# One block of attention products a pair in place of three, between the units of a Strassen MLP

## The chip, the cores and the metric

The kernel runs on one core of a Trainium2 chip. The metric is the device time of one execution in microseconds (us), as the median of several runs. A profile is one execution with the hardware profiler on; it gives a start and a duration for each instruction of each engine: TensorE (PE, and PEld for its weight loads), VectorE (DVE), ScalarE (ACT), GpSimd (POOL), SyncE (SP, which here issues DMAs).

## What is computed

A retention layer (attention without softmax, with a decay per head) feeds an MLP with a PReLU.

```python
# q, k, v: (8 batches, 8 heads, 576 positions, 64), all fp32
scores = q @ k.T / 8
ret = scores * where(i >= j, gamma[h] ** (i - j), 0)
x = (ret @ v), heads side by side            # (4608 tokens, 512)
h = x @ w_in                                 # (4608, 2048)
out = (max(h, 0) + alpha * min(h, 0)) @ w_out  # (4608, 512)
```

## The kernel before

**Attention.** Two heads make a pair; a batch has 4 pairs, so there are 32 of them, numbered n. A sequence is cut into 9 chunks of 64 positions. Inside a chunk the retention is worked out from scores; what lies in earlier chunks comes through a running state, a 64 x 64 sum of k and v products per head, decayed from chunk to chunk. A pair therefore has these steps:

- `load_pair`: SP loads `kx`, `qx` (to be transposed), `kn` and `vn`; two buffers of each.
- `scale_pair`: decay factors go onto `qx` (POOL, line 524) and `vn` (ScalarE, 529). `transposes`: `kT`, `qT` on VectorE (535).
- `pair_scores`: 18 products `kT` by `qT` into PSUM tiles `ps` (552); ScalarE copies `qT` into `mt` (555); VectorE masks the scores into `mt` (560).
- `pair_states`: 16 products `kn` by `vn` into `pu` (571); ScalarE copies and VectorE adds up the running sums `su` (576 to 584). `pair_sums` copies `su` into the free half of `vn` (590).
- `pair_values`: 18 products of `vn` (values and sums, 128 rows) by `mt` (chunk scores and q, 128 rows) into `pv` (601); ScalarE copies `pv` into the MLP's input `xb` (610). One product thus yields the chunk's own part and that of the state.

Scores and states are 64*64 products that use quarters of TensorE's array, values are 128*64, MLP products 128*128. In fp32 one product is two instructions on TensorE.

**MLP.** 256 tokens make a block kb. From block 2 on, each of both matrix products is a 2 x 2 block product in 7 products with sums and differences of the operands (Strassen-Winograd); `combine_x` makes those of `xb` on POOL (449). A block has 8 units. A unit (`mlp_unit`) has 28 instructions into the PSUM tiles `ph` with tags `psh0` and `psh1` (line 463), then VectorE turns `ph` into `g` (474 to 485), and `mlp_out` issues the 14 instructions of the unit before it into `po` (381). After a block's last unit `out_block` adds `po` up on VectorE (367, 368) and SP sends two DMAs of 128 rows (371).

**PSUM** has 8 banks: two for attention (tag `psa`, through `ps_tile`), one each for `psh0` and `psh1`, four for `po`.

**Order.** The first 157 us (batches 0 and 1, blocks 0 and 1, and the preparation of the weights) are written out by hand under `manual_schedule`; there, too, pairs 4 to 7 go through the functions above. Then `queue` holds the MLP units that are ready, and a loop over the 24 pairs of batches 2 to 7 issues scores, some units, states, some units, transposes of the next pair and values, some units (`cuts` has the numbers; 2, 1 and 1 as a rule). A scheduler places these instructions on their engines; TensorE's come out in the order of the program, VectorE's nearly so. After a batch, `enqueue(b)` adds the blocks that it completed, so each batch's attention runs between the MLP units of the batch before it. The last 24 units have no attention beside them.

Of the kernel before, what the change touches and what calls it, by code (L numbers as in the profile page):

```python
# [18 lines left out]
def kernel(  # L19
# [49 lines left out]
    def half(x):  # L69
        return slice(x * C, (x + 1) * C)  # L70
# [36 lines left out]
    def load_pair(n):  # L107
        b, c = pairs[n]
        kx, qx, kn = [nat.tile([P, S], FP32, tag=t, name=f"{t}_{n}") for t in ("kx", "qx", "kn")]
        kx, qx = [t.rearrange("p (n r) -> p n r", r=32) for t in (kx, qx)]  # L110
        kn = kn.rearrange("p (j d) -> p j d", d=D)
        vn = nat.tile([P, 2, NJ, D], FP32, tag="vn", name=f"vn_{n}")
        load_sq(kx, k, b, c)
        load_sq(qx, q, b, c)
        for t, src in ((vn, v), (kn, k)):
            for h2 in range(2):
                load_head(t[half(1 - h2), h2] if t is vn else t[half(1 - h2)], src, b, 2 * c + h2)
        for h2 in range(2):

            nc.scalar.copy(vn[half(h2), h2, 0], zero[half(h2)])  # L120
        return kn, kx, qx, vn
# [233 lines left out]
    def out_block(kb, po):  # L355
        p1, p2, p6, p7, p5, p3, p4 = [po[n // 2][:, n % 2, :] for n in range(7)]

        osb = ring.tile([P, 2, 2, HM], FP32, tag=f"o{kb % 2}", name=f"osb_{kb}")
        s12 = wraw.tile([P, 2, HM], FP32, tag="wa", name=f"s12_{kb}")
        u3 = wraw.tile([P, HM], FP32, tag="wa", name=f"u3_{kb}")  # L360
        s1, u2 = s12[:, 0], s12[:, 1]
        nc.scalar.copy(s1, p1)
        for o, x, y, op in ((osb[:, 0, 0], p2, s1, ALU.add), (u2, p6, s1, ALU.add),
                            (u3, p7, u2, ALU.add), (s1, p5, u2, ALU.add),
                            (osb[:, 1, 1], p5, u3, ALU.add),
                            (osb[:, 0, 1], p3, s1, ALU.add)):
            nc.vector.tensor_tensor(out=o, in0=x, in1=y, op=op)  # L367
        nc.vector.tensor_tensor(out=osb[:, 1, 0], in0=p4, in1=u3, op=ALU.add)
        for m in range(2):
            t0 = kb * TB + m * P  # L370
            nc.sync.dma_start(out[t0:t0 + P, :], osb[:, m].rearrange("p x f -> p (x f)"))
# [134 lines left out]
    def pop_units(n):  # L506
        for _ in range(min(n, len(queue))):
            kb, i = queue.pop(0)
            mlp_unit(kb, i)
            if i == NU // 2 and kb + 1 < NKB and ready[kb + 1] <= done[0]:  # L510
                combine_x(kb + 1)
# [5 lines left out]
    def ps_tile(shape, name):  # L517
        return ps_a.tile(shape, FP32, tag="psa", name=name)

    def scale_pair(n):  # L520
        c = pairs[n][1]
        qx, vn = loaded[n][2:]
        qh = qx.rearrange("p (j x) r -> p j x r", x=2)
        nc.gpsimd.tensor_tensor(out=qh, in0=qh,  # L524
                                in1=tabx[:, None, c, :, None].to_broadcast([P, NJ, 2, 32]),
                                op=ALU.mult)
        for h2 in range(2):
            x = half(1 - h2)
            nc.scalar.activation(vn[x, h2], vn[x, h2], ACTF.Copy, scale=tabv[x, c:c + 1])  # L529

    def transposes(n):
        kT = attn.tile([P, S], FP32, tag="kT", name=f"kT_{n}")
        qT = attn.tile([P, S], FP32, tag="qT", name=f"qT_{n}")
        for src, dst in ((loaded[n][1], kT), (loaded[n][2], qT)):
            nc.vector.transpose(dst, src.rearrange("p n r -> p (n r)"))
        return kT, qT

    def chunk(j):
        return slice(j * C, (j + 1) * C)
# [3 lines left out]
    def pair_scores(n, kT, qT):  # L543
        c = pairs[n][1]

        mt = attn.tile([P, 2 * S], FP32, tag="at", name=f"mt_{n}").rearrange(
            "p (h j s) -> p h j s", h=2, s=C)
        ps = [ps_tile([P, NM, C], f"ps{p2}_{n}") for p2 in range(2)]
        for j in range(NJ):
            for h2 in range(2):  # L550
                x = (1 - h2, h2)[j % 2]
                nc.tensor.matmul(ps[j % 2][half(x), j // 2], kT[half(h2), chunk(j)],  # L552
                                 qT[half(h2), chunk(j)], start=True, stop=True)
        for h2 in range(2):
            nc.scalar.copy(mt[half(h2), h2].rearrange("p j s -> p (j s)"), qT[half(h2)])
        for p2 in range(2):
            for h2 in range(2):
                h, to, x = 2 * c + h2, half(1 - h2), (1 - h2, h2)[p2]
                nm = NM - p2
                nc.vector.scalar_tensor_tensor(  # L560
                    out=mt[to, h2, p2::2], in0=ps[p2][half(x), 0:nm], scalar=th[to, 3, h:h + 1],
                    in1=mask[to, None, :].to_broadcast([C, nm, C]), op0=ALU.mult, op1=ALU.mult)
        return mt

    def pair_states(n, kn, vn):
        c = pairs[n][1]
        ps = [ps_tile([P, NM - 1, D], f"pu{p2}_{n}") for p2 in range(2)]
        for j in range(NJ - 1):
            for h2 in range(2):
                x = (h2, 1 - h2)[j % 2]  # L570
                nc.tensor.matmul(ps[j % 2][half(x), j // 2], kn[half(1 - h2), j],  # L571
                                 vn[half(1 - h2), h2, j], start=True, stop=True)
        su = attn.tile([P, S], FP32, tag="kT", name=f"su_{n}")[:, 0:S - D].rearrange(
            "p (j d) -> p j d", d=D)
        g1, g2 = gch[:, 0, c:c + 1], gch[:, 1, c:c + 1]
        nc.scalar.copy(su[:, 0::2], ps[0])
        for h2 in range(2):
            nc.vector.scalar_tensor_tensor(
                out=su[half(h2), 1::2], in0=su[half(h2), 0::2], scalar=g1[half(h2)],
                in1=ps[1][half(1 - h2)], op0=ALU.mult, op1=ALU.add)  # L580
        for j in range(3, NJ - 1, 2):
            nc.vector.scalar_tensor_tensor(out=su[:, j], in0=su[:, j - 2], scalar=g2,
                                           in1=su[:, j], op0=ALU.mult, op1=ALU.add)
        nc.vector.scalar_tensor_tensor(out=su[:, 2::2], in0=su[:, 1:NJ - 3:2], scalar=g1,  # L584
                                       in1=ps[0][:, 1:], op0=ALU.mult, op1=ALU.add)
        return su

    def pair_sums(vn, su):
        for h2 in range(2):
            nc.scalar.copy(vn[half(h2), h2, 1:], su[half(h2)])  # L590

    def pair_values(n, vn, mt):
        b, c = pairs[n]
        w = TB // C

        j1 = -b * NJ % w or w
        j1 += w if NJ - j1 > 6 else 0
        pv = [ps_tile([P, (j1, NJ - j1)[i], C], f"pv{i}_{n}") for i in range(2)]
        for j in range(NJ):
            for h2 in range(2):  # L600
                nc.tensor.matmul(pv[j >= j1][half(h2), j - (j1 if j >= j1 else 0)],  # L601
                                 vn[:, h2, j], mt[:, h2, j], start=True, stop=True)
        j = 0
        while j < NJ:
            kb, o = divmod(b * NJ + j, w)
            if kb not in xb:
                xb[kb] = ring.tile([P, NCC, TB], FP32, tag=f"x{kb % NRING}", name=f"xb_{kb}")
            m, i = min(w - o, NJ - j), j >= j1
            j0 = j - (j1 if i else 0)
            nc.scalar.copy(xb[kb][:, c, o * C:(o + m) * C].rearrange("p (j s) -> p j s", s=C),  # L610
                           pv[i][:, j0:j0 + m])
            j += m
# [276 lines left out]
    enqueue(0)  # L889
    enqueue(1)  # L890

    for n, (b, c) in enumerate(pairs):
        if n <= last:
            continue
        if n == last + 1:
            pop_units(1)
        if n + 1 < len(pairs) and n + 1 not in loaded:
            loaded[n + 1] = load_pair(n + 1)
        kn, _, _, vn = loaded[n]
        share = -(-len(queue) // (NPAIR - c))  # L900
        cuts = [(share + i) // 3 for i in range(3)][::-1]
        kT, qT = turned.pop(n)
        mt = pair_scores(n, kT, qT)
        pop_units(cuts[0])
        pair_sums(vn, pair_states(n, kn, vn))
        pop_units(cuts[1])
        if n + 1 < len(pairs):
            scale_pair(n + 1)
            turned[n + 1] = transposes(n + 1)
        pair_values(n, vn, mt)  # L910
        del loaded[n]
        pop_units(cuts[2])
        if c == NPAIR - 1:
            enqueue(b)
    pop_units(len(queue))
    while pend:
        mlp_out()
# [28 lines left out]
```

## Time and profile before

| | |
|---|---|
| median of 12 runs | 1025.8 us (1024.52 to 1027.35) |
| profiled execution | 1025.64 us, of which the span of instructions is 1023.9 us |
| granted TensorE clock | 0.996 |
| PE busy | 1008.5 us, 98% |
| DVE busy | 768.0 us, 75% |
| ACT busy | 268.9 us |
| POOL busy | 179.2 us |

The span runs from the first to the last instruction; the run's time is 1.7 us longer. "Busy" sums the durations of an engine's instructions, and matmuls overlap, so a PE busy share near 100% says that TensorE nearly always had work in flight, not that it ran at its peak. Which engine sets the end is read from the chain that ended last: it follows the last instruction back, step by step, to what released it.

### The profile page before, as it was taken

The numbers are of one execution on the slowest core, as the hardware profiler recorded it, in microseconds if no ns is written. First come the engines' busy times: TensorE is split into PE (matmuls) and PEld (weight loads), VectorE is DVE, ScalarE is ACT, GpSimd is POOL, SyncE is SP. The second block draws the span as 40 slices with busy tenths as digits, with TensorE's granted clock in tenths as the row PEclk, the third lists the DMA queues.
The fourth block names the chain that finished last, engine by engine and source line by source line (L and its number), as shares of the span: only waits on it lengthen the run. The fifth ranks groups of instructions, "written<-read, shape, count | busy, mean of one in ns | idle before, by whom it ended". The sixth has DMA issues, their size and how long they took to land.

```text
span 1023.9 us, 23109 instructions
## 1 busy us (share of the span) xinstructions
PE 1008.5 (98%) x9385; PEld 890.9 (87%) x9385; DVE 768.0 (75%) x2038; ACT 268.9 (26%) x605; POOL 179.2 (17%) x201
## 2 busy tenths in 40 slices
PE   6999999999999999999999999999999999999998
PEld 5766668999999999999999999999999999999997
DVE  6769967787878787776868787878787777667665
ACT  4656652223222222122122221222222211000000
POOL 5656675200200010100010000200020001010000
PEclk8999999999999999999999999999999999999999
DMA  9975743223323222112113222222222100000000
GB/s 240 241 190 147 185 77 90 48 57 59 67 38 67 48 47 56 25 47 45 40 30 67 48 55 43 63 48 56 48 48 57 24 22 2 22 1 21 1 21 22
DMA packets 229307, 64.30 MB, mean 63 GB/s; under 512 B 214336, under 2 KB 222544, under 8 KB 229200
## 3 DMA queue, kind: packets, MB, share of 16 engines
q1 hardware_dynamic: 227088, 62.29, 26.8%
q8 instruction: 74, 1.21, 0.5%
q10 hardware_dynamic: 2112, 0.53, 0.3%
q14 instruction: 33, 0.27, 0.1%
HBM read 53.35 MB, written 9.44 MB: 61 GB/s over the span
## 4 chain that ended last, share of the span: by engine, by line
PE 98%; DMA 1%; DVE 0%; issue 0%; ACT 0%; SPq 0%; DVEq 0%
PE ph L463 40%; PE po L381 38%; PE ph L419 6%; PE po L398 6%; PE pv L601 3%; PE ps L552 2%; PE pu L571 2%; DMA w_out<-in_k_dram 1%; PE pt L642 0%; PE pv L720 0%; PE ps L661 0%; PE pv L709 0%; DVE pa L668 0%; PE pu L681 0%; DVE s L367 0%
## 5 line engine op out<-in xcount | busy, mean ns | idle before, releaser
L381 PE MATMUL po<-w_out,g 128*128 128x256 f32 x1792 | 407.8, 379 | 0.0
L381 PEld LDWEIGHTS po<-w_out,g 128*128 128x128 f32 x1792 | 330.8, 190 | 39.7
L474 DVE TENSOR_TENSOR g<-ph,g 128x256 f32<-128x256 f32 (+1 forms) x512 | 187.9, 388 | 184.4 <-ACT g L469 112.6
L463 PE MATMUL ph<-xb,w_in 128*128 128x128 f32 x2048 | 277.7, 279 | 0.0
L463 PEld LDWEIGHTS ph<-xb,w_in 128*128 128x128 f32 x2048 | 253.1, 192 | 8.2 <-issue 0.5
L463 PE MATMUL ph<-xt,w_in 128*128 128x128 f32 x1536 | 213.3, 275 | 0.0
L463 PEld LDWEIGHTS ph<-xt,w_in 128*128 128x128 f32 x1536 | 192.1, 192 | 0.0
L469 ACT COPY g<-ph 128x128 f32<-128x128 f32 x128 | 33.9, 265 | 396.4 <-PE ph L463 374.3
L485 DVE TENSOR_TENSOR g<-g 128x128 f32<-128x128 f32 x512 | 126.9, 289 | 7.8
L479 DVE SCALAR_TENSOR_TENSOR g<-g 128x512 f32<-128x512 f32 x128 | 91.8, 717 | 3.9
L477 DVE TENSOR_SCALAR g<-g,alpha 128x256 f32<-128x256 f32 x256 | 85.0, 374 | 3.7
L524 POOL TENSOR_TENSOR qx<-qx,tabx 128x576 f32<-128x576 f32 x28 | 32.9, 1174 | 309.8 <-DMA qx<-in_q_dram 254.6
L419 PE MATMUL ph<-xb,w_in 128*128 128x256 f32 x256 | 61.6, 397 | 0.8 <-ACT xb L728 0.8
L560 DVE SCALAR_TENSOR_TENSOR mt<-ps,th,mask 64x320 f32<-64x320 f32 (+1 forms) x112 | 57.8, 516 | 4.5 <-PE ps L552 2.7
L419 PEld LDWEIGHTS ph<-xb,w_in 128*128 128x128 f32 x256 | 50.0, 198 | 11.0 <-issue 3.2
L398 PE MATMUL po<-w_out,g 128*128 128x512 f32 x128 | 58.6, 599 | 0.9 <-DVE g L435 0.9
L449 POOL TENSOR_TENSOR xt<-xb 128x256 f32<-128x256 f32 x16 | 11.6, 727 | 214.7 <-PE ph L463 202.4
L449 POOL TENSOR_TENSOR xt<-xb,xt 128x256 f32<-128x256 f32 x32 | 23.6, 738 | 143.0 <-ACT xb L610 142.3
L529 ACT ACTIVATE vn<-vn,tabv 64x576 f32<-64x576 f32 x56 | 43.3, 773 | 15.3 <-DMA vn<-in_v_dram 14.7
L398 PEld LDWEIGHTS po<-w_out,g 128*128 128x128 f32 x128 | 23.4, 190 | 24.5 <-issue 22.9
L590 ACT COPY vn<-su 64x512 f32<-64x512 f32 x56 | 34.5, 616 | 37.8 <-DVE su L584 37.2
L610 ACT COPY xb<-pv 128x256 f32<-128x256 f32 (+3 forms) x84 | 22.6, 321 | 78.8 <-PE pv L601 78.7
(122 smaller groups left out, 688.6 us busy)
## 6 DMA issues: line engine op xcount, KB each, us to landing
out_dram<-osb SPq DMA_DIRECT2D x36, 256.0 KB, 2.3
kx<-in_k_dram SPq DMA_DIRECT2D x112, 72.0 KB, 2.6
qx<-in_q_dram SPq DMA_DIRECT2D x112, 72.0 KB, 2.5
vn<-in_v_dram SPq DMA_DIRECT2D x56, 144.0 KB, 3.2
kn<-in_k_dram SPq DMA_DIRECT2D x56, 144.0 KB, 3.2
raw<-in_moe_w_in_dram SPq DMA_DIRECT2D x24, 256.0 KB, 4.1
raw<-in_moe_w_out_dram SPq DMA_DIRECT2D x10, 512.0 KB, 4.6
w_in<-in_moe_w_out_dram SPq DMA_DIRECT2D x6, 512.0 KB, 5.6
```

The source lines that it names most:

```text
L381: nc.tensor.matmul(acc[kb][n // 2][:, n % 2, :], g[:, x, :], w_out[i][:, y, :], start=(i == 0 and n % 2 == 0), stop=(i == NU - 1 and (n % ...
L398: nc.tensor.matmul(acc[kb][m], g[:, 2 * x + m], w_out[i][:, 2 * x:2 * x + 2].rearrange("p x f -> p (x f)"), start=(i == 0 and x == 0), sto ...
L419: nc.tensor.matmul(ph[:, x], w_in[i // UST][:, cc // 2 * 2 + x, i % UST, cc % 2], xb[kb][:, cc], start=(cc == 0 and x == 0), stop=(cc == N ...
L449: nc.gpsimd.tensor_tensor(out=o, in0=x0, in1=x1, op=ALU.subtract)
L463: nc.tensor.matmul(ph[m][:, o], w_in[i // UST][:, l, i % UST, cc], r[:, cc], start=(n in (0, 3) and cc == 0), stop=(n in (2, 6) and cc == ...
L474: nc.vector.tensor_tensor(out=o, in0=x0, in1=x1, op=ALU.add)
L477: nc.vector.tensor_scalar(g[:, 4 + 2 * m:6 + 2 * m], g[:, 2 * m:2 * m + 2], 0.0, alpha[:, fc:fc + 1], ALU.min, ALU.mult)
L479: nc.vector.scalar_tensor_tensor(out=g[:, 0:4].rearrange("p x t -> p (x t)"), in0=g[:, 0:4].rearrange("p x t -> p (x t)"), scalar=0.0, in1 ...
L485: ins = nc.vector.tensor_tensor(out=g[:, o, :], in0=g[:, x0, :], in1=g[:, x1, :], op=op)
L529: nc.scalar.activation(vn[x, h2], vn[x, h2], ACTF.Copy, scale=tabv[x, c:c + 1])
L560: nc.vector.scalar_tensor_tensor(out=mt[to, h2, p2::2], in0=ps[p2][half(x), 0:nm], scalar=th[to, 3, h:h + 1], in1=mask[to, None, :].to_bro ...
L590: nc.scalar.copy(vn[half(h2), h2, 1:], su[half(h2)])
```

## The change

The loop over pairs gives way to a loop over units, which calls `joint(n)` after 25 of them.

- `joint(n)` issues the values of pair n-1, then one last score chunk of pair n, then (in `pair_front`) the other 16 score products and the 16 state products of pair n, all in one stretch on TensorE.
- Values and the last score chunk go into tiles of the tags `psh0` and `psh1`, which are those of `ph`; `extra` is the last 64 columns of the second one. Scores and states of a pair share two banks of `psa`.
- `pair_front` traces the copies of `qT` into `mt`, the two masks of the last chunk and the four others. The running sums (`running_sums`, split out of `pair_states`, and `pair_sums`) and the scaling and transposes of the next pair (`operands`) go into the list `later`; the loop takes one entry after each unit, though none after the first unit of a block.
- The places: with nq units in a batch's queue, units c * nq // 4 + 2 for c = 0 to 3, counted from 0 and moved one on from a multiple of 8. That is 2, 6, 10, 14 for 16 units and 2, 9, 14, 20 for 24; the first batch's loop has 0, 3, 6, 10, 14.
- The last block's output goes out in four DMAs of 128 rows by 256 columns, two on SP and two on ScalarE's queue.

```diff
+        if kb == NKB - 1:
+            for (m, x), eng in (((0, 0), nc.sync), ((1, 1), nc.scalar), ((0, 1), nc.sync),
+                                ((1, 0), nc.scalar)):
+                t0 = kb * TB + m * P
+                eng.dma_start(out[t0:t0 + P, x * HM:(x + 1) * HM], osb[:, m, x])
+            return
...
+    later = []
+    def pair_front(n, kT, qT, kn, vn, extra):
+        c = pairs[n][1]
+        mts[n] = mt = attn.tile([P, 2 * S], FP32, tag="at", name=f"mt_{n}").rearrange(
+            "p (h j s) -> p h j s", h=2, s=C)
+        ps = [ps_tile([P, 2, NM - 1, C], f"ps{p2}_{n}") for p2 in range(2)]
+        for j in range(NJ - 1):
+            for h2 in range(2):
+                x = half((1 - h2, h2)[j % 2])
+                nc.tensor.matmul(ps[j % 2][x, 0, j // 2],
+                                 kT[half(h2), chunk(j)], qT[half(h2), chunk(j)],
+                                 start=True, stop=True, skip_group_check=True)
+        for j in range(NJ - 1):
+            for h2 in range(2):
+                x = half((h2, 1 - h2)[j % 2])
+                nc.tensor.matmul(ps[j % 2][x, 1, j // 2], kn[half(1 - h2), j],
+                                 vn[half(1 - h2), h2, j], start=True, stop=True,
+                                 skip_group_check=True)
+        for h2 in range(2):
+            nc.scalar.copy(mt[half(h2), h2].rearrange("p j s -> p (j s)"), qT[half(h2)])
+        for h2 in range(2):
+            to = half(1 - h2)
+            nc.vector.scalar_tensor_tensor(
+                out=mt[to, h2, NJ - 1], in0=extra[to],
+                scalar=th[to, 3, 2 * c + h2:2 * c + h2 + 1], in1=mask[to],
+                op0=ALU.mult, op1=ALU.mult)
+        for p2 in range(2):
+            for h2 in range(2):
+                h, to, x = 2 * c + h2, half(1 - h2), (1 - h2, h2)[p2]
+                nc.vector.scalar_tensor_tensor(
+                    out=mt[to, h2, p2:NJ - 1:2], in0=ps[p2][half(x), 0],
+                    scalar=th[to, 3, h:h + 1],
+                    in1=mask[to, None, :].to_broadcast([C, NM - 1, C]),
+                    op0=ALU.mult, op1=ALU.mult)
+        later.append(lambda: pair_sums(vn, running_sums(n, ps[0][:, 1], ps[1][:, 1])))
...
     def pair_values(n, vn, mt, pv=None, then=None):
...
+        if then:
+            then()
...
+    def operands(n):
+        scale_pair(n)
+        turned[n] = transposes(n)
+
+    def joint(n):
+        pv = [ps_h.tile([P, 8, C], FP32, tag=f"psh{m}", name=f"pv{m}_{n}") for m in range(2)]
+        extra = pv[1][:, 7]
+        def last_chunk():
+            if n < len(pairs):
+                kT, qT = turned[n]
+                for h2 in range(2):
+                    nc.tensor.matmul(extra[half(1 - h2)], kT[half(h2), chunk(NJ - 1)],
+                                     qT[half(h2), chunk(NJ - 1)], start=True, stop=True)
+        if n - 1 in mts:
+            pair_values(n - 1, loaded.pop(n - 1)[3], mts.pop(n - 1), pv, last_chunk)
+        else:
+            last_chunk()
+        if n == len(pairs):
+            return
+        pair_front(n, *turned.pop(n), loaded[n][0], loaded[n][3], extra)
+        if n + 1 < len(pairs):
+            if n + 1 not in loaded:
+                loaded[n + 1] = load_pair(n + 1)
+            later.append(lambda: operands(n + 1))
+
+    mts.clear()
+    n = 2 * NPAIR
+    for b in range(2, B):
+        nq = len(queue)
+        at = [u + (u % NU == 0) for u in (c * nq // NPAIR + 2 for c in range(NPAIR))]
+        if b == 2:
+            at = [0, 3] + at[1:]
+        for u in range(nq):
+            first = queue[0][1] == 0
             pop_units(1)
+            if later and not first:
+                later.pop(0)()
+            if u in at:
+                assert not later
+                joint(n)
+                n += 1
+        enqueue(b)
```

More of the change, by code (lines that the diff above doesn't have):

```diff
@@ L565, in pair_states @@
     def pair_states(n, kn, vn):
-        c = pairs[n][1]
         ps = [ps_tile([P, NM - 1, D], f"pu{p2}_{n}") for p2 in range(2)]
@@ L572, in pair_states, with running_sums @@
                                  vn[half(1 - h2), h2, j], start=True, stop=True)
+        return running_sums(n, *ps)
+    def running_sums(n, even, odd):
+        c = pairs[n][1]
         su = attn.tile([P, S], FP32, tag="kT", name=f"su_{n}")[:, 0:S - D].rearrange(
@@ L575, in pair_states @@
         g1, g2 = gch[:, 0, c:c + 1], gch[:, 1, c:c + 1]
-        nc.scalar.copy(su[:, 0::2], ps[0])
+        nc.scalar.copy(su[:, 0::2], even)
         for h2 in range(2):
@@ L579, in pair_states @@
                 out=su[half(h2), 1::2], in0=su[half(h2), 0::2], scalar=g1[half(h2)],
-                in1=ps[1][half(1 - h2)], op0=ALU.mult, op1=ALU.add)
+                in1=odd[half(1 - h2)], op0=ALU.mult, op1=ALU.add)
         for j in range(3, NJ - 1, 2):
@@ L584, in pair_states @@
         nc.vector.scalar_tensor_tensor(out=su[:, 2::2], in0=su[:, 1:NJ - 3:2], scalar=g1,
-                                       in1=ps[0][:, 1:], op0=ALU.mult, op1=ALU.add)
+                                       in1=even[:, 1:], op0=ALU.mult, op1=ALU.add)
         return su
@@ L590, in pair_sums, with pair_values @@
             nc.scalar.copy(vn[half(h2), h2, 1:], su[half(h2)])
-    def pair_values(n, vn, mt):
+    later = []
+    def pair_front(n, kT, qT, kn, vn, extra):
+        c = pairs[n][1]
+        mts[n] = mt = attn.tile([P, 2 * S], FP32, tag="at", name=f"mt_{n}").rearrange(
+            "p (h j s) -> p h j s", h=2, s=C)
+        assert C == D and NJ == 9
+        ps = [ps_tile([P, 2, NM - 1, C], f"ps{p2}_{n}") for p2 in range(2)]
[28 more added lines that the diff above has]
+        later.append(lambda: pair_sums(vn, running_sums(n, ps[0][:, 1], ps[1][:, 1])))
+    def pair_values(n, vn, mt, pv=None, then=None):
         b, c = pairs[n]
@@ L597, in pair_values @@
         j1 += w if NJ - j1 > 6 else 0
-        pv = [ps_tile([P, (j1, NJ - j1)[i], C], f"pv{i}_{n}") for i in range(2)]
+        pv = pv or [ps_tile([P, (j1, NJ - j1)[i], C], f"pv{i}_{n}") for i in range(2)]
         for j in range(NJ):
@@ L890 @@
     enqueue(1)
[L892 to L895, printed above, removed]
-            pop_units(1)
[L897 to L914, printed above, removed]
+    def operands(n):
[30 more added lines that the diff above has]
+            first = queue[0][1] == 0
+            pop_units(1)
+            if later and not first:
[5 more added lines that the diff above has]
+        enqueue(b)
+    assert n == len(pairs) + 1
     pop_units(len(queue))
```

## The prediction

> **What bounds the kernel now.** I read the page first: the engines' shares and the chain that ended last.
>
> ```profile
> PE 1008.5 (98%) x9385; PEld 890.9 (87%) x9385; DVE 768.0 (75%) x2038; ACT 268.9 (26%) x605; POOL 179.2 (17%) x201
> PE 98%; DMA 1%; DVE 0%; issue 0%; ACT 0%; SPq 0%; DVEq 0%
> ```
>
> The chain is TensorE for 98% of the span. So a microsecond is won only where TensorE has less to do or wastes less between its instructions, and lost where it is made to wait. Next I read the chain in order of time, around two pairs in the middle of the kernel (start us, us, what).
>
> ```profile
> 518.68 3.02 PE po L381 x14
> 521.70 1.20 PE pv L601 x36
> 522.90 3.32 PE ph L463 x28
> 526.22 3.02 PE po L381 x14
> 529.25 3.12 PE ph L463 x28
> 532.37 3.02 PE po L381 x14
> 535.39 0.73 PE ps L552 x36
> 536.12 3.32 PE ph L463 x28
> ...
> 548.62 0.62 PE pu L571 x32
> 549.24 3.32 PE ph L463 x28
> ```
>
> The reader is to see that the pieces touch: no wait stands between them. An MLP unit is 3.12 + 3.02 = 6.14 us. Each pair cuts in three times: scores (ps), states (pu), values (pv). After each of these the `ph` piece takes 3.32 instead of 3.12, so a cut costs 0.20 us more than its own piece: scores 0.93, states 0.82, values 1.40, **3.15 us a pair**. With 24 pairs in this part that is 75.6 us.
>
> How much of it is products, and how much stopping and starting? The early stage has blocks of 64*64 products of another length (PE timeline: start, us, group).
>
> ```profile
> 37.65 1.16 PE L709 MATMUL pv<-w_out,w_out 64*64 64x64 f32 x64
> 38.74 0.36 PE L720 MATMUL pv<-w_out,w_out 64*32 64x64 f32 x11
> 52.84 0.68 PE L756 MATMUL pv<-w_out,w_out 64*64 64x64 f32 x16
> 53.45 0.65 PE L763 MATMUL pv<-w_out,w_out 64*32 64x64 f32 x32
> ```
>
> From the start of L709 to the start of L720, 64 instructions take 1.09 us. The 32 of a states block take 0.62 to the start of the next piece. Both begin after 128*128 work and end at a change of tile shape, so 32 more instructions are worth 0.47 us. The states block is therefore 0.47 of products and 0.82 - 0.47 = **0.35 us of restart**. I take the same restart for the other two.
>
> **What the Trainium skill says.** TensorEngine Tiling (Array Packing), Key Properties: changing the tiling mode, and not just the tile, drains TensorE. The 0.35 us around each block agree. PSUM — Partial Sum Buffer, Terms: two engines on one bank and quadrant at once is an error. So readers and writers of a bank have to take turns; no wait in this trace shows it, but it matters below, because the change puts values into the two banks of `ph`. DMA: Bandwidth & Descriptors, Anatomy of one DMA: about 2.0 us fixed plus bytes at 436 GB/s. That is an estimate of 2.6 us for 256 KB; the trace has 2.3 us to landing for the output.
>
> **The change, part by part.**
>
> TensorE, the order. The loop now calls `joint` at units 0, 3, 6, 10, 14 of the first batch's queue, and 2, 6, 10, 14 of a queue of 16 or 2, 9, 14, 20 of one of 24: 25 calls for 72 blocks. Most issue values of pair n-1, one last score chunk of pair n (4 instructions), 32 of scores, 32 of states. Nothing is computed less.
> - Values with their own restart: 1.40 (row above).
> - Change of shape from 128*64 to 64*64 inside the block: not in the trace before. The nearest rows are 64*64 to 64*32: 1.09 us less 64 instructions at 0.47/32 (0.94) leaves 0.15. Bounds: nothing, if this direction is free, and a whole restart, 0.35. I take 0.15.
> - Last chunk: scores minus states today, 0.93 - 0.82 = 0.11.
> - Scores and states: 0.47 each. No restart between them: both are 64*64.
>
> A full call is 1.40 + 0.15 + 0.11 + 0.94 = 2.60 us. There are 23 of them, 59.8. The first has no values (0.11 + 0.94 + 0.35 = 1.40), the last only values (1.40). Sum 62.6 against 75.6: **13.0 us saved**. Bounds from the shape change: 23 x 0.15 = 3.4 more, or 23 x 0.20 = 4.6 less.
>
> New waits at a call. (1) Values now write the banks of `ph`, which VectorE must have read. A unit in VectorE's timeline:
>
> ```profile
> 551.21 0.42 DVE L474 TENSOR_TENSOR g<-ph,g 128x256 f32<-128x256 f32 x1
> 552.60 1.08 DVE L474 TENSOR_TENSOR g<-ph,g 128x256 f32<-128x256 f32 x3 [0.45 <-PE ph L463]
> 555.63 1.02 DVE L485 TENSOR_TENSOR g<-g 128x128 f32<-128x128 f32 x4
> ```
>
> Its `ph` piece ended at 552.56; the banks were read by 553.68, 1.1 us later, while `po` runs 3.02. Covered by 1.9 us. (2) The next unit's `ph` waits for the copies of values out of these banks: before, they end 1.74 us after the values begin (ScalarE's last L610 group, 522.95 + 0.49 against 521.70). It also waits for VectorE's two reads of the last chunk in the second bank. The call lasts 2.4 us to the first `ph`, which needs the second bank only 12 instructions (1.3 us) later. VectorE is done with the unit 4.1 us after its `ph` (556.65 against 552.56), 1.1 into the call; its two reads come first in the program and can follow the copies at 1.74, to end near 2.4 (0.3 each, my estimate between the 0.29 of a 128x128 row and the 0.48 of a 64x256 one). Covered by about 1.3 us. I cost both at nothing.
>
> VectorE, moved work. A unit's own work is 4.0 us (545.60 to 549.64 in its timeline). The call's unit gets four masks of 0.48 and two of 0.3: 2.5, so 6.5 in 6.14 + 2.60. The next unit gets the sums: 2 x 0.48 + 3 x 0.33 + 0.41 = 2.4, so 6.4 in 6.14; 0.3 us late, made good by the one after, 4.0 + two transposes of 0.77 = 5.5. A first unit of a block has the seven output sums (2.9) and none of the pair's work. TensorE needs `g` one piece later: in the fence 556.65 against the next `po` at 560.10. Nothing on the path.
>
> ScalarE, POOL, queues. ScalarE keeps its copies (0.96 of values, 1.34 of `mt`, 0.37 and 1.23 of sums, 1.55 of scaling a pair) in units where it is otherwise busy 0.27 us. POOL's 1.17 us scaling waits on loads, two units (12 us) after SP issues them, landing in 2.5 to 3.2 us behind twelve issues of about 0.5 (four `kx` in 1.94). Behind them on SP stand only outputs. `combine_x` (4 x 0.74 on POOL) for a batch's first block starts after the last call's copies, with one whole unit between: 3 us of 6.1. Nothing.
>
> The tail. Today the last rows go out so:
>
> ```profile
> 1019.10 0.41 DVE L367 TENSOR_TENSOR osb<-po,s 128x256 f32<-128x256 f32 x1
> 1019.43 0.41 DVE L368 TENSOR_TENSOR osb<-po,u 128x256 f32<-128x256 f32 x1
> 1019.54 1.06 SPq L371 DMA_DIRECT2D out_dram<-osb  x2
> ```
>
> Then four DMAs of half the size go out over two queues; the last waits for L368 alone and carries 128 KB less, about 0.3 us at the skill's rate, and isn't behind the other on SP. I take 0.4; bounds -0.3 (two more DMAs, shorter rows) to 0.8.
>
> Sum: 13.0 + 0.4 = 13.4 us off the profiled execution's 1025.64 (span 1023.9), so 1012.2; the median, 1025.8, lies 0.16 above it: **1012.4**.
>
> **Rivals.**
> - A, slower: VectorE's two reads of the last chunk fall behind the masks in its order. Masks can start when the states are written, 2.5 us into the call, and take 1.9, the reads 0.6: 5.0, where `ph` wants the bank at 3.7: 1.3 us at each of 24 calls, 31 us against 13.4, **1043**. It decides from 0.56 us a call. For it: VectorE's order is not that of the program (a transpose stands between two L474 today). Against it: the reads are traced first and are ready first.
> - B: the order is broken. kT and qT are late and a unit slips between values and scores, or the shape change costs a whole restart: 23 x 0.20 less, **1017.0**. Against it: today all 72 blocks stand where the program puts them.
> - C: the change does not do what it says, and scores and states restart too: 23 x 0.55 less, 12.7, hardly anything but the tail is left, **1025**. Against it: L661 and L681, both 64*64, follow each other in the early stage without a gap.
>
> **How the numbers follow.** The forecast has 0.78, B 0.12, C 0.04, A 0.06. About 0.2% (2 us) can be told from no change. Forecast and B give faster, 0.90; C the same, 0.04; A slower, 0.06. The forecast's own bounds are 1025.8 - 13.0 - 3.4 - 0.8 = 1008.6 and 1025.8 - 13.0 + 4.6 + 0.3 = 1017.7; 0.1 us of waiting at each call would add 2.4. The range is 1008.5 to 1020; it holds B and leaves out A and C.
>
> **What would show it.** In the chain after: pv (36), then ps and pu with no `ph` between, about 2.4 us together, once in 4 to 7 units; `ph` at 3.32 only 25 times; no idle time before `ph`. DVE busy up by about 0.5 us a pair. Wrong if PE waits for `xb` copies (ACT) or `mt` (DVE) ahead of `ph`, if `ph` stands between pv and ps, or if the block lasts over 2.8 us.

## The result, and the profile after

The changed kernel takes **1011.4 us** (median of 7 runs, 1010.32 to 1012.84) against 1025.6 for the one before (29 runs): ratio 0.9864, interval 0.9854 to 0.9873. Forecast were 1012.4 us and 1008.5 to 1020. The profiled execution has a span of 1009.8 us, 14.1 less than before.

The page of the kernel after, the lines that answer to those of before:

```profile
PE 993.8 (98%) x9385; PEld 890.9 (88%) x9385; DVE 770.7 (76%) x2086; ACT 267.3 (26%) x605; POOL 178.8 (18%) x201
PE 95%; DMA 2%; DVE 1%; SPq 1%; issue 0%; ACT 0%; DVEq 0%; ACTq 0%
```

TensorE issues the same 9385 instructions and is still the chain (the DMA and SP shares in it lie in the opening stage). The change took 14 us out of its stream and nothing out of its work. The chain in order of time (start us, us, what) around one call of `joint`:

```profile
506.25 3.02 PE po L388 x14
509.27 1.20 PE pv L652 x36
510.47 0.20 PE pv L961 x2
510.67 0.03 PE ps L616 x2
510.70 0.03 PE pv L961 x2
510.73 0.46 PE ps L616 x27
511.19 0.47 PE ps L622 x32
511.67 3.32 PE ph L470 x28
514.99 3.02 PE po L388 x14
```

Values (L652), last chunk (L961, its second half between the first scores), scores (L616) and states (L622) touch each other and the units on both sides. The block is 2.39 us, and 0.20 more sits in the first `ph` after it: 2.59, where 3.15 stood. The 0.20 at the head of L961 holds the change of tile shape and part of the last chunk; between L616 and L622, both 64*64 products, nothing is lost.

The weight loads (PEld) show the same from another side: in this part they stand idle for 0.33 us just before each block of small products. One of three such rows before, and the main row after (weight load, waited for: us in total, times, longest):

```profile
PEld pu L571 <- issue: 8.0, 24, 0.3
```

```profile
PEld pv L652 <- DVE g L492: 7.6, 23, 0.3
```

Before, the rows of scores, states and values have 72 such pauses together, one a block; after, there are 25, one a call. The row after names a line of VectorE, but the pause is no longer than before.

**Where the 14 us lie.** Three stretches can be cut at TensorE's own marks: the start of the first Strassen `ph`, and the start of the last 28 `po` instructions (PE timeline; before, then after).

```profile
152.78 1.05 PE L463 MATMUL ph<-xb,w_in 128*128 128x128 f32 x8
...
1012.62 6.21 PE L381 MATMUL po<-w_out,g 128*128 128x256 f32 x28
```

```profile
152.94 1.05 PE L470 MATMUL ph<-xb,w_in 128*128 128x128 f32 x8
...
999.70 6.21 PE L388 MATMUL po<-w_out,g 128*128 128x256 f32 x28
```

| stretch | before | after | saved | forecast |
|---|---|---|---|---|
| opening stage | 152.8 | 152.9 | -0.2 | 0 |
| loop with the pairs' blocks | 859.83 | 846.75 | 13.1 | 13.0 |
| tail (to the end of the span) | 11.3 | 10.1 | 1.2 | 0.4 |

The opening stage varies between profiles of kernels that do not change it (151.9 to 155.2 over this study), more than the small effects below. The loop is the same to 0.01 us in every profile of an unchanged loop: 859.83 in four, 846.75 in two. So I compare loops and tails below, and give the run times beside them.

### The profile page after: what moved, and what is told of

It is laid out like the page before. It is cut to its first block, busy times and chain, and to the rows that moved or that the text cites. A ratio compares the mean times of both kernels' runs of the same rounds, so it can differ in the third digit from the quotient of the medians.

```text
span 1009.8 us, 23126 instructions
## 1 busy us (share of the span) xinstructions
PE 993.8 (98%) x9385; PEld 890.9 (88%) x9385; DVE 770.7 (76%) x2086; ACT 267.3 (26%) x605; POOL 178.8 (18%) x201
## 4 chain that ended last, share of the span: by engine, by line
PE 95%; DMA 2%; DVE 1%; SPq 1%; issue 0%; ACT 0%; DVEq 0%; ACTq 0%
PE ph L470 40%; PE po L388 38%; PE po L405 5%; PE ph L426 5%; PE pv L652 3%; PE ps L616 1%; PE ps L622 1%; DMA raw<-in_moe_w_in_dram 1%; DMA raw<-in_moe_w_out_dram 1%; DMA w_out<-in_v_dram 1%; SPq L78 1%; PE pv L961 1%; PE ps L559 0%; PE pu L577 0%; DVE wc L310 0%
## 5 line engine op out<-in xcount | busy, mean ns | idle before, releaser
L470 PE MATMUL ph<-xb,w_in 128*128 128x128 f32 x2048 | 272.7, 276 | 0.0
L470 PEld LDWEIGHTS ph<-xb,w_in 128*128 128x128 f32 x2048 | 257.1, 192 | 7.4 <-issue 0.5
L470 PE MATMUL ph<-xt,w_in 128*128 128x128 f32 x1536 | 213.3, 275 | 0.0
L470 PEld LDWEIGHTS ph<-xt,w_in 128*128 128x128 f32 x1536 | 192.1, 192 | 0.0
L426 PE MATMUL ph<-xb,w_in 128*128 128x256 f32 x256 | 58.9, 383 | 1.7 <-issue 0.9
L426 PEld LDWEIGHTS ph<-xb,w_in 128*128 128x128 f32 x256 | 47.8, 190 | 11.3 <-issue 4.5
L636 DVE SCALAR_TENSOR_TENSOR mt<-ps,th,mask 64x256 f32<-64x256 f32 x96 | 46.4, 483 | 2.2
L629 DVE SCALAR_TENSOR_TENSOR mt<-pv,th,mask 64x64 f32<-64x64 f32 x48 | 13.6, 283 | 40.1 <-ACT xb L663 39.7
```

The source lines that it names most:

```text
L426: nc.tensor.matmul(ph[:, x], w_in[i // UST][:, cc // 2 * 2 + x, i % UST, cc % 2], xb[kb][:, cc], start=(cc == 0 and x == 0), stop=(cc == N ...
L470: nc.tensor.matmul(ph[m][:, o], w_in[i // UST][:, l, i % UST, cc], r[:, cc], start=(n in (0, 3) and cc == 0), stop=(n in (2, 6) and cc == ...
L636: nc.vector.scalar_tensor_tensor(out=mt[to, h2, p2:NJ - 1:2], in0=ps[p2][half(x), 0], scalar=th[to, 3, h:h + 1], in1=mask[to, None, :].to_ ...
```

## The experiments

Theory: the gain is restarts, 0.35 us each time TensorE leaves 128*128 work for small products and comes back, and TensorE never waits at a call. Rivals: fewer waits rather than fewer restarts; a shape change as dear as a restart; a cover at the `ph` banks that is really there or not.

**Each half alone.** `joint_only` is the change without its first hunk, the four output DMAs; `tail_only` is the kernel before with that hunk.

> The changed loop without the four output DMAs at the end. My theory (the TensorE stream got 12.9 us shorter and the tail gave 1.2 us more): ratio to before 0.9874, that is about 12.9 us less, and from the start of the last 28 po instructions to the end of the span 11.2 to 11.3 us as before. Rival (the tail is worth the 0.4 us of the prediction and the rest of the 14.2 us came from the blocks): about 13.8 us less and a last stretch of about 10.5 us.

Loop 846.75, tail 11.29 us; 1014.2 us, ratio 0.987 (0.984 to 0.990).

> The kernel before with the four output DMAs alone. My theory: last stretch (start of the last 28 po instructions to the end of the span) 10.1 us instead of 11.3, ratio 0.9988. Rival (0.4 us as predicted): 10.9 us, ratio 0.9996.

Loop 859.83, tail 10.10 us; 1025.0 us, ratio 0.9984 (0.9973 to 0.9995). The halves add up: 13.1 and 1.2. The tail's part was three times the 0.4 of the forecast.

**The tail taken apart**, on the kernel before. `tail_two_queues` has this edit; `tail_four_sp` has the change's four DMAs, all on `nc.sync`.

```diff
+        if kb == NKB - 1:
+            for m, eng in enumerate((nc.sync, nc.scalar)):
+                t0 = kb * TB + m * P
+                eng.dma_start(out[t0:t0 + P, :], osb[:, m].rearrange("p x f -> p (x f)"))
+            return
```

> The kernel before; the last block's two DMAs keep their 256 KB, but the second goes out on ScalarE's queue instead of behind the first on SP. If the gain is the queue: the last stretch falls by 0.5 us or more, to at most 10.8 us. If it is that half of the bytes leave earlier: it stays within 0.3 us of 11.3.

> The kernel before; the last block's output as four DMAs of 128 KB in the order of the change, all on SP. If the gain is that bytes leave earlier and the last DMA is small: last stretch 10.1 to 10.5 us. If it is the second queue: 11 us or more.

Tails 11.11 and 10.26 us; 1026.0 us (ratio 0.9995, 0.998 to 1.0009) and 1024.9 us (0.9989, 0.998 to 0.9999). By these tails the second queue alone gave 0.2, the quarters alone 1.0, both together 1.2. They do not price the queue, as the DMA view of the last microseconds shows. Its row GB/s has what moved in each of 40 slices of the window; below it stands the time from issue to landing of the last DMA. In order: before, `tail_two_queues` (slices of 0.1 us), after, and `values_last` (0.0875 us), a later kernel with the change's four DMAs.

```profile
GB/s 0 0 0 123 328 348 389 369 430 348 246 226 471 410 307 410 348 369 103 41 20 20 20 0 0 0 0 0 0 0 0 0 0 0 0 0 0 0 0 0
q14 instruction: 1, 0.01, 0.5%
out_dram<-osb SPq DMA_DIRECT2D x1, 256.0 KB, 2.5
```

```profile
GB/s 0 0 0 0 0 20 348 389 348 369 389 451 369 369 328 410 369 451 369 226 41 0 0 0 0 0 0 0 0 0 0 0 0 0 0 82 0 0 0 0
out_dram<-osb ACTq DMA_DIRECT2D x1, 256.0 KB, 2.4
```

```profile
GB/s 0 0 0 0 0 0 0 12 234 328 374 351 340 328 374 328 328 351 363 304 316 152 12 0 0 0 0 0 0 0 0 0 0 0 0 0 0 0 0 0
out_dram<-osb ACTq DMA_DIRECT2D x2, 128.0 KB, 1.8
```

```profile
GB/s 211 328 374 374 328 328 363 363 293 328 316 316 293 153 105 0 0 12 23 12 12 23 12 0 0 0 0 0 0 0 0 0 0 0 0 0 0 0 0 0
q14 instruction: 1, 0.01, 0.5%
out_dram<-osb ACTq DMA_DIRECT2D x1, 128.0 KB, 2.7
```

Every one of these programs has one packet of 8 KB on the instruction queue (q14) near its end, each at another moment. Before and in `values_last` it falls among the last bytes of the output, and the transfer ends with single packets, for 0.4 us before (41, 20, 20, 20) and 0.7 us in `values_last`. After, it falls between the bytes of the first output DMA and those of the second (1006.26 to 1006.65 us; the bytes shown begin at 1007.2), and in `tail_two_queues` behind all of them (the 82); there the transfer has no such end. `values_last` has a tail of 10.95 us; the seven other kernels with its output code, in which the packet falls as after, have 10.10 or 10.11. That the packet holds back the single packets is inferred from where it falls; no run moved the packet alone.

So the 0.2 of `tail_two_queues` is two things. Its last DMA lands 0.53 us earlier than before (9.66 us after the tail's start against 10.19), but the program then ends 1.45 us after that landing, where it is 1.11 before and 0.98 after: the instruction packet, itself 0.38 us long, stands at the very end there. That it delays the end is inferred.

The 1.2 of the change are three steps of the trace. VectorE is done 7.23 us after the tail's start in both kernels. The last DMA is issued at 7.26 in place of 7.66 (0.40), lands 1.87 us later in place of 2.52 (0.65, in which the packet has a share that these runs do not isolate), and the end follows 0.98 us after that in place of 1.11 (0.13).

**Restarts.** `split_su` issues the states as a block of their own one unit after the scores. `split_v` issues the values one unit ahead (the last three lines).

```diff
-        for j in range(NJ - 1):
+        def states():
+            for j in range(NJ - 1):
...
+        later.append(states)
...
+            if u + 1 in at:
+                values(n)
             if u in at:
```

> The changed kernel with the 32 state products as a block of their own, one unit after the scores; nothing else moves but the sums, which follow one unit later. My theory (a block that starts and stops between 128*128 products costs 0.35 us of restart, and scores and states side by side cost none): 24 restarts more, 8.3 us, the loop from the first Strassen ph to the last 28 po instructions 855.0 us instead of 846.75. Rival (scores and states restart in one block too, so that the gain came from fewer or cheaper waits): no change, 846.8.

Loop 855.29 us, 8.54 more; 1019.1 us, ratio 0.9936 (0.9921 to 0.9951). The chain of `split_su`:

```profile
513.95 0.47 PE ps L616 x28
514.42 3.32 PE ph L470 x28
517.74 3.02 PE po L388 x14
520.76 0.62 PE ps L623 x32
521.39 3.32 PE ph L470 x28
```

The states' 0.47 have become 0.62, and a second `ph` has 3.32. A restart is 8.54 / 24 = 0.356 us. The rival with waits has nothing to show here: no wait was added.

> The changed kernel with the values of pair n-1 one unit ahead, as a block of their own, still in the banks of ph. Theory from the trace after (restart 0.35, shape change inside the block 0.20): 23 x 0.15 = 3.4 us more, loop 850.2 us. By the prediction's terms (0.35 and 0.15): 4.6 us, 851.4. If the shape change inside the block costs as much as a restart: 846.8.

Loop 853.10 us, 6.35 more; 1018.0 us, ratio 0.9925 (0.991 to 0.994). More than any of the three. The waits of TensorE name a part of it, one wait in the first Strassen block (engine, line, waited for: us, times, longest):

```profile
PE po L388 <- DVE g L486: 1.7, 1, 1.7
```

The rest, 4.7, is the split. In its chain the block without values is

```profile
516.88 0.20 PE px L962 x2
517.08 0.03 PE ps L616 x2
517.11 0.03 PE px L962 x2
517.14 0.46 PE ps L616 x27
517.60 0.47 PE ps L622 x32
518.07 3.32 PE ph L470 x28
```

1.19 + 0.20 = 1.39 us, beside values at 1.40: 2.79 against 2.59 in one block, 0.20 x 23 = 4.6. With a restart of 0.356 that makes the shape change 0.356 - 0.20 = 0.16. My 0.20 for it, from the head of L961, was wrong: part of that piece belongs to the last chunk, whose four instructions cost 0.1. The prediction's 0.15 and 0.11 came out.

There is a simpler way to count, and it is an estimate from these runs. A block alone changes the tile shape twice, on the way in and on the way out; the states taken out in `split_su` add two changes and 0.356 us, the values taken out in `split_v` add one and 0.20. A change of shape is thus worth 0.16 to 0.20 us here. A pair had six of them before and has three in one call, and the saving of a pair is 3.15 - 2.59 = 0.56.

**The direction of the shape change.** `values_last` has the values after the states.

> The changed kernel with the values of pair n-1 at the end of the block, after last chunk, scores and states: the shape changes from 64*64 to 128*64 in place of the other way round. If the shape change costs the same both ways and no wait is new: within 1 us of 1011.4, loop 846 to 848. If the other way is cheaper (0.15 us, the price of the prediction): 1 us less. If ph then waits for the copies of the values, which end 1.74 us after the values' start against 1.3 for the first bank of ph: up to 0.5 us at 23 places, 11 us more.

Loop 847.20 us, 0.45 more; 1013.6 us, ratio 0.9884 (0.9869 to 0.9899). The three changes of shape of a block cost the same in either order, to 0.02 us a call; no run isolates one change in one direction. TensorE waited nowhere in the loop, but the scheduler has put two `po` instructions (0.43 us) between the first and the second bank of `ph` there, so it is not shown that the copies would have been in time in the program's own order. The rest of the 2 us is the tail above and the opening stage.

**The cover at the `ph` banks.** `extras_fixed` puts VectorE's two reads of the last chunk behind the four masks by a dependency, and `po` behind `ph`. `extras_late` has the first dependency only.

```diff
+                last_mask = nc.vector.scalar_tensor_tensor(
+                    out=mt[to, h2, p2:NJ - 1:2], in0=ps[p2][half(x), 0],
...
+            ins = nc.vector.scalar_tensor_tensor(
+                out=mt[to, h2, NJ - 1], in0=extra[to],
...
+            tc.add_manual_dep(ins.ins, last_mask.ins.name, mybir.DependencyInfo(
+                mybir.DependencyClass.Sync, mybir.DependencyReason.DATA),
```

> The changed kernel with VectorE's two reads of the last score chunk ordered behind the four masks, and each unit's po ordered behind its ph as it stands in the changed kernel. The prediction's rival A: the reads end 5.0 us or more after the block's start, ph wants the bank at 3.83, TensorE waits 1.2 us or more at 24 places, 29 us in all, 1040 us. If the cover was larger than I think (ph doesn't wait for these reads): no change, 1011.5 us.

1115.5 us, ratio 1.0864 (1.0836 to 1.0893); loop 949.16, 102.4 more, **4.3 us a call** on the average of 24. The mechanism of rival A is there, and dearer than it had it. The chain around one call of `extras_fixed`:

```profile
518.58 1.22 PE pv L661 x36
519.82 0.67 ACT mt L632
520.49 0.38 ACT xb L672 x2
520.89 0.68 ACT mt L632
521.65 0.78 DVE qT L548
522.46 0.49 DVE mt L636
...
525.17 0.29 DVE mt L643
525.59 3.53 PE ph L476 x16
```

Behind the values stand two copies of `qT` into `mt` (ScalarE), then VectorE's transpose of the next `qT`, which waits for them, then the masks, then the two reads (L643). They end 6.9 us after the block's start, not 5.0: TensorE waits 3.1. After this wait 16 instructions of `ph` take 3.53 us, twice their usual 1.8, and the mean granted clock from 519 to 530 us is 0.84 where it is 1.00 on both sides. That is not so at every call. The trace has 22 waits of 3.0 to 3.2 us for these reads; the granted clock falls to 0.5, for 3.4 or 6.8 us, at 13 of them and stays at 1.00 at the nine others (at 281.7 us the 16 instructions after the wait take 2.02). All waits in the loop are 71 us of the 102; most of the other 31 fits the 58 us at half clock. The order of `po` alone, without the late reads, was not run.

> The changed kernel with VectorE's two reads of the last chunk behind the four masks, TensorE's order left to the scheduler, which puts 8 of the 14 po instructions between the first and the second bank of ph. If the wait of the kernel with the fixed order (3.3 us) is shortened by what those 8 instructions take, 1.7 us: 1.6 us at 24 places, 38 us, and less of it if the clock stays up: about 1050 us. If po fills it whole: 1012 us.

1048.2 us, ratio 1.0218 (1.0198 to 1.0237); loop 883.45, 36.7 more. The scheduler fills part of the gap with `po`; 1.5 us a call are left, of which the waits themselves are 1.3 to 1.5, with the clock at 1.00 throughout the loop. This is rival A as the prediction had it, with TensorE's order left free: 1043 us were forecast for it.

In the changed kernel itself (its timeline):

```profile
510.52 0.67 ACT L626 COPY mt<-qT 64x576 f32<-64x576 f32 x1 [0.21 <-PE pv L652]
511.10 0.47 ACT L663 COPY xb<-pv 128x256 f32<-128x256 f32 x2
511.60 0.58 DVE L629 SCALAR_TENSOR_TENSOR mt<-pv,th,mask 64x64 f32<-64x64 f32 x2 [1.79 <-ACT xb L663]
512.59 1.06 PE L470 MATMUL ph<-xt,w_in 128*128 128x128 f32 x8
```

A copy of `qT` stands between the copies of the values, so the second bank's copies end at 511.57 and the reads at 512.18, 2.98 us into the block, which begins at 509.20 in this view. The second bank of `ph` starts at 3.83 (among the L470 that begin at 512.59). The cover is 0.8 us (0.7 to 0.9 over the calls), not the 1.3 of the forecast.

**A version that beats both.** Chunk 0 has no state, so half of its value product multiplies zeros. `chunk0_small` issues it as 64*64 products and turns the last score chunk to the other diagonal.

```diff
-        for j in range(NJ):
+        for j in range(1 if then else 0, NJ):
...
         if then:
+            for h2 in range(2):
+                nc.tensor.matmul(pv[0][half(h2), 0], vn[half(1 - h2), h2, 0],
+                                 mt[half(1 - h2), h2, 0], start=True, stop=True)
             then()
...
-                    nc.tensor.matmul(extra[half(1 - h2)], kT[half(h2), chunk(NJ - 1)],
+                    nc.tensor.matmul(extra[half(h2)], kT[half(h2), chunk(NJ - 1)],
```

> The changed kernel with the values of chunk 0, whose state half is all zeros, as 64*64 products at the end of the values, and the last score chunk turned to the other diagonal of the array, so that both can run at once in different banks. By the prediction's prices: values lose 0.12 us, the two chunks together take 0.12 in place of 0.10 for the last score chunk alone, 0.10 us less at 23 places, 2.3 us: loop 844.5 us in place of 846.75, 1009.1 us. Rival (chunk 0 and the last score chunk run one after the other): no gain, loop 846.8 or 847.

Loop 844.52 us; 1009.6 us, ratio 0.9846 (0.9832 to 0.986). Its chain:

```profile
507.53 1.08 PE pv L652 x32
508.61 0.20 PE pv L656 x2
508.81 0.01 PE pv L964 x2
508.83 0.04 PE pv L656 x2
508.87 0.01 PE pv L964 x2
508.89 0.47 PE ps L616 x32
```

The instructions of chunk 0 (L656) and of the last score chunk (L964) alternate, and the second pair of each adds only 0.04 and 0.01 us. The loop fell by 2.23 us against 2.3 by the prices and nothing by the rival, so the two ran at once.

## Why the prediction was right, point by point

- **The bound**: TensorE's stream, with no wait in it. Held; after the change no wait of TensorE stands in the loop either, and 72 blocks became 25.
- **Restart 0.35**: 0.356 by `split_su`.
- **Shape change 0.15**: 0.16 by `split_v`. This was in part luck. The 0.15 was read as a change from 64*64 to 64*32, but 1.09 - 0.94 is the same number as 0.62 - 0.47 by the way in which the 0.47 was found. It is what either block spends beside its products, so part of the restart itself, and no measurement of another change of shape.
- **Last chunk 0.11, scores and states side by side**: the block without values is 1.39 us, forecast for the first call 1.40.
- **A full call 2.60, saved 13.0**: 2.59, and 13.1 in the loop.
- **The tail, 0.4**: the term that was mis-sized. It was 1.2, beyond its bounds of -0.3 to 0.8, and makes most of the forecast's miss of 1.0 us. The earlier issue alone gave 0.40, and the last DMA landed 0.65 sooner after it, where 0.3 stood for its 128 KB. That 0.3 is an estimate from the rate in the Trainium skill (DMA: Bandwidth & Descriptors, Anatomy of one DMA), which gives it for DMAs issued by GpSimd; these go out on SP's and ScalarE's queues. Put at nothing was the instruction packet, which goes with 0.4 us of single packets before and with none after; how much of the 0.65 it is stays open.
- **No new wait**: right in the outcome, with a cover of 0.8 us where I had 1.3. The term that failed is the end of the copies, 1.74 us after the values' start; it was 2.4 (511.57 against 509.20), as ScalarE's order has a `qT` copy between them.
- **VectorE, ScalarE, POOL, SP**: hidden as forecast. Each of the two new reads takes 0.28 us (0.3 estimated); they add 13.6 us (48 of L629), near the 0.5 a pair of the forecast. The four masks lose 3.2 (49.6 to 46.4), and DVE busy, which counts overlapping records once, rose by 2.7 in all: the forecast's sign, busy up by 0.5 a pair, did not come.
- **Rival A**: did not come in the changed kernel; two kernels brought it about by a dependency. Its price was 31 us. With TensorE's order free it is 36.7, which is near, but by two errors that offset each other: the reads end 6.9 us into the block and not 5.0, and the scheduler fills 1.7 us of the wait with `po`. With `po` held back it is 102. **B**: the order held; splitting values from the rest costs 4.7 beside the one wait, and B had 4.6. **C**: refuted by the chain after and by `split_su`.

## What to carry to other kernels

Where TensorE is the chain and its pieces touch, count how often the tile shape changes between the pieces. Take two block lengths of the same product and solve for the fixed part; that price can then be counted per block, and merging blocks pays it once. When merged work borrows a buffer of the main stream, write down when its last reader ends and when the stream wants it back, with the order of that reader's engine and not only its durations.

## What the runs showed that I had not expected

Waits of 3.1 us cost TensorE 4.3 on average: at 13 of 22 the granted clock fell to half for 3.4 or 6.8 us, and at nine of the same length it did not. Waits of up to 1.5 us left the clock at 1.00. And one packet of the instruction queue among the last bytes of the output goes with a last DMA that lands 0.8 us later (2.70 against 1.87 us).
